# A delta rule with a gated feed-forward behind it, on one core: the same instructions issued in another order

## The chip, the cores and the metric

The kernel runs on one core of a Trainium2 chip. A core has a matrix engine (PE, with PEld for its weight loads), a vector engine (DVE), a scalar engine (ACT), GpSimd (POOL) and a queue engine (SP); DMAs are issued from the streams of SP, ACT and POOL. Every engine takes its instructions in the order in which the program gives them, and waits where one is not ready. The metric is the device time of one execution in microseconds (us); the kernel before takes 507.92 us (median of 3 runs, 506.95 to 509.35).

## The reference

The inputs are q, k, v of shape 4 x 8 x 768 x 48 (batch, head, token, channel) and beta of 4 x 8 x 768. For each of the 32 heads, token by token:

```
k_n = k / (norm(k) + 1e-6);  state = 0
y[t]  = q[t] @ state
state = state + beta[t] * outer(k_n[t], v[t] - k_n[t] @ state)
```

The heads' y, put side by side, is x (4 x 768 x 384). Behind it stands a feed-forward with gating over tokens:

```
h = gelu(x @ w_in)                      # 384 -> 1024; u, v = the two halves of 512
v_n = (v - mean) / sqrt(var + 1e-6) * g_ln
v_s = w_sg @ v_n + b_sg                 # over the 768 tokens
out = x + (u * v_s) @ w_out             # 512 -> 384
```

## The kernel before

The recurrence is worked out in 12 chunks (0 to 11) of 64 tokens: chunks 0 to 5 for two of the batches, 6 to 11 for the other two. Within a chunk one needs the inverse of a triangular 64 x 64 matrix for each head. The program has a step for each piece of work, and the string PROGRAM (lines 47 to 98) names the steps one after the other; the loop at line 1128 calls them, and each engine gets its instructions in just that order. Nothing else sets the order. Of a step `name:a:b` the numbers say which chunk, part or queue; S, A and P are the DMA queues of SP, ACT and POOL.

- **Loads and Gram matrices.** `keys`, `q`, `kt`, `v` load a chunk's arrays; `w:k` loads a piece of w_in (six pieces; the later three are loaded from POOL when an earlier piece is done, line 768). `gram:c` multiplies a chunk's keys with each other (line 129, as all the recurrence's matmuls), and `gstore` sends the result to DRAM (gd).
- **Lanes.** The inverse of the 32 x 32 blocks is made on DVE, row by row, in four groups: group 0 for chunks 0 and 1, group 1 for chunks 2 and 3, group 2 for chunks 4 to 7, group 3 for chunks 8 to 11. `lanes:0` issues the whole of group 0 at once, behind `tin`, which brings the blocks in with a DVE transpose. `bglanes:g` only puts a later group's instructions on a list, and `l:n` issues the next n of them. A group begins with a copy of the diagonal (line 351) and a masking on POOL (line 353); the pairs at lines 407 and 414 are its bulk. `zload` fetches a group's blocks from gd into the one tile zl; at a group's end the result is stored to DRAM (zd, line 461), and `blocks` and `heads` load it back (line 467).
- **Chain of a chunk.** `join`, `corner_a`, `corner_b` put the 32 x 32 blocks together on PE, with ACT copying out of PSUM. Then, twice a chunk (e = 0, 1): `old` (PE; DVE adds to v at line 638 and masks gq at line 322), `own` (PE, ACT), `state` (PE, ACT). The next half needs the state of the one before.
- **Decoding.** w_in arrives as 64-bit words and is taken apart on DVE into a high and a low float: `d:n` issues the next n of 18 parts, three for each of the six pieces, with 4, 3 and 2 DVE instructions and one ACT cast (lines 719 to 737). `gate` needs the first three pieces, `values` all six.
- **First feed-forward.** For each chunk `turn` transposes x, `gate:c:d` makes a quarter of u (9 matmuls, lines 775 to 777, and a gelu on ACT), and `values:c:n` issues the next n of 18 matmuls of v (line 811); at the 9th and the 18th follow the gelu, a store to DRAM (vD) and the moments on DVE. This is the work with which PE can be filled while a chain waits.
- **Weights of the second part.** `late_weights` and 22 `unit` steps load and split w_out and w_sg.
- **Second part.** From `last_part` on: `vload` and `vsplit` load v from vD and normalize and split it (ACT, DVE), `sp` (18 matmuls, then DVE, then POOL) and `gs` (split) do the mixing over tokens, `pj` (12 matmuls) the projection, `xload` and `ost` are its load and store. For batches 1 and 3 the split v is put where winh and winl lie.
- **Warming.** `kick`, `warm` and `wm` issue matmuls whose results nobody reads.

The steps that begin the kernel before, and its third-last stage, read:

```
kick:12 consts beta:P l:7 keys:0:S ... gram:1 w:0:P keys:3:P tin l:12 wm:9:13 d:3 lanes:0 keys:2:A
gram:3 gram:2 ... zload:1:S old:0:0 ... bglanes:1 heads:0 wm:6:7 join:0:0 ...
... unit:1 l:2 values:11:18
vsplit:0:3 unit:1 vsplit:0:4 vsplit:0:5 unit:1 norm ... sp:0:0:0
```

Of the kernel before, what the change touches and what calls it, by code (L numbers as in the profile page):

```python
# [48 lines left out]
gram:3 gram:2 l:3 wm:2:3 gstore:2:S:S q:0:P norms:0 v:0:P vprep:0 q:1:S gstore:3:P zload:1:S old:0:0 keys:4:S keys:5:P
blocks:0:P kt:0:A bglanes:1 heads:0 wm:6:7 join:0:0 keys:7:S join:1:0 turned:0 l:5 l:8 l:1 l:5 blocks:1:P w:2:S gram:4  # L50
gstore:4:S:P w:1:P join:2:0 join:3:0 warm:6 l:8 l:8 heads:1:A corner_a:0 v:1:P l:5 l:7 gram:5 corner_b:0 join:0:1
kt:1:P turned:1 join:1:1 l:5 l:4 keys:6:S d:1 vprep:1 own:0:0 l:12 gstore:5:S:A state:0:0 old:1:0 join:2:1 keys:8:P
own:1:0 d:4 join:3:1 state:1:0 d:1 gram:6 blocks:2:S:S:P zload:2:S corner_a:1 xstore:0 old:0:1 heads:2:S:P join:0:2
corner_b:1 d:1 own:0:1 l:5 d:2 d:1 gram:7 l:2 gstore:6:A:P:A join:1:2 turned:2 l:3 gstore:7:S:P:P d:2 d:1 state:0:1
join:2:2 zload:3:P old:1:1 norms:1 join:3:2 d:2 v:2:S bglanes:2 own:1:1 turn:0 keys:10:A l:6 vprep:2 heads:3:P q:2:S
l:2 gram:8 state:1:1 corner_a:2 gate:0:0 keys:9:A blocks:3:S:S corner_b:2 l:13 old:0:2 l:2 l:1 kt:2:S join:0:3 l:2
join:1:3 turned:3 values:0:4 l:7 values:0:2 own:0:2 values:0:6 xstore:1 values:0:6 gram:9 state:0:2 l:6 turn:1
join:2:3 v:3:P gstore:8:P old:1:2 keys:11:A vprep:3 l:5 gate:0:1 kt:3:P gate:0:2 join:3:3 q:3:A own:1:2 corner_a:3 l:5
values:1:10 values:1:3 state:1:2 xstore:2 l:5 q:4:S values:1:2 gate:1:0 old:0:3 l:1 l:9 corner_b:3 norms:2 gate:0:3
ustore:0 own:0:3 values:1:3 state:0:3 gstore:9:A turn:2 old:1:3 gate:1:1 gate:1:2 kt:4:P v:4:S l:1 gate:1:3 own:1:3  # L60
ustore:1 gram:10 q:5:S gate:2:0 gstore:10:S:A gate:2:1 heads:4:P state:1:3 gram:11 values:2:2 blocks:4:S:A gate:2:2
l:10 gate:2:3 gstore:11:S:P v:5:P zload:4:S vprep:4 values:2:1 turn:3 zload:5:P bglanes:3 values:2:7 blocks:5:S:P
gate:3:0 old:0:4 corner_a:4 values:2:1 values:2:5 turned:4 corner_b:4 values:2:2 heads:5:P gate:3:1 own:0:4 gate:3:2
vprep:5 gate:3:3 ustore:2 state:0:4 l:12 old:1:4 turned:5 corner_a:5 own:1:4 heads:6:S:A:P blocks:6:P v:6:A values:3:1
state:1:4 ustore:3 corner_b:5 values:3:1 l:15 values:3:13 l:1 old:0:5 xstore:4 turn:4 l:4 kt:5:A values:3:2 values:3:1
l:3 kt:6:A own:0:5 turned:6 xstore:3 l:2 values:4:7 values:4:11 state:0:5 norms:3 corner_a:6 vprep:6 old:1:5
heads:7:S:S gate:4:0 corner_b:6 q:6:S own:1:5 norms:4 gate:4:1 blocks:7:S state:1:5 l:11 old:0:6 own:0:6 norms:5
gate:4:2 v:7:S l:1 gate:4:3 turn:5 l:2 state:0:6 turned:7 corner_a:7 l:3 gate:5:0 old:1:6 l:4 ustore:4 l:1 gate:5:1
xstore:5 own:1:6 gate:5:2 q:7:S l:7 l:2 values:5:3 values:5:15 q:8:S vprep:7 l:1 state:1:6 xstore:6 kt:7:A v:8:P
corner_b:7 old:0:7 kt:8:P gate:5:3 ustore:5 turn:6 l:12 blocks:8:S l:7 heads:8:S own:0:7 values:6:18 state:0:7  # L70
gate:6:0 bgnorm old:1:7 gate:6:1 turned:8 vprep:8 own:1:7 gate:6:2 state:1:7 unit:1 corner_a:8 gate:6:3 v:9:P old:0:8
q:9:P corner_b:8 turn:7 own:0:8 gate:7:0 gate:7:1 late_weights heads:9:A l:6 kt:9:S gate:7:2 unit:1 state:0:8
blocks:9:S gate:7:3 old:1:8 turned:9 corner_a:9 own:1:8 heads:10:A values:7:4 ustore:6 ustore:7 unit:1 values:7:4
blocks:10:S:A state:1:8 corner_b:9 vprep:9 v:10:A old:0:9 values:7:6 turn:8 own:0:9 l:1 values:7:3 xstore:7 turned:10
values:7:1 gate:8:0 unit:1 state:0:9 vprep:10 corner_a:10 old:1:9 q:10:S gate:8:1 gate:8:2 heads:11:P:A own:1:9
gate:8:3 unit:1 state:1:9 unit:1 xstore:8 blocks:11:P corner_b:10 ustore:8 turn:9 l:7 kt:10:P old:0:10 values:8:18
own:0:10 values:9:5 unit:1 l:10 v:11:A state:0:10 unit:1 q:11:P turned:11 gate:9:0 xstore:9 old:1:10 gate:9:1 gate:9:2
unit:1 corner_a:11 own:1:10 values:9:6 unit:1 values:9:7 vprep:11 state:1:10 corner_b:11 old:0:11 kt:11:P turn:10
gate:9:3 values:10:5 values:10:4 own:0:11 values:10:3 unit:1 unit:1 l:4 unit:1 state:0:11 values:10:6 old:1:11
xstore:10 gate:10:0 own:1:11 unit:1 gate:10:1 ustore:9 state:1:11 unit:1 xstore:11 turn:11 gate:10:2 gate:10:3 l:15  # L80
gate:11:0 gate:11:1 last_part vload:0:0 vload:0:1 unit:1 l:5 vload:0:2 uload:0:0 vload:0:3 vsplit:0:0 vload:0:4 unit:1
gate:11:2 vsplit:0:1 gate:11:3 vload:0:5 gains unit:1 ustore:11 vsplit:0:2 ustore:10 unit:1 l:2 values:11:18
vsplit:0:3 unit:1 vsplit:0:4 vsplit:0:5 unit:1 norm uload:0:1 vload:1:0 unit:1 vload:1:1 vload:1:2 vload:1:3 sp:0:0:0
sp:0:0:1 gs:0:0:0 vsplit:1:0 vload:1:4 sp:0:0:2 gs:0:0:1 vsplit:1:1 vload:1:5 sp:0:0:3 gs:0:0:2 vsplit:1:2 gs:0:0:3
sp:0:1:0 vsplit:1:3 sp:0:1:1 gs:0:1:0 sp:0:1:2 gs:0:1:1 vsplit:1:4 uload:1:0 sp:0:1:3 vsplit:1:5 gs:0:1:2 xload:0:0
xload:0:1 xload:0:2 gs:0:1:3 pj:0:0 ost:0:0 pj:0:1 ost:0:1 pj:0:2 ost:0:2 vload:2:0 vload:2:1 vload:2:2 l:1 vload:2:3
sp:1:0:0 sp:1:0:1 gs:1:0:0 vsplit:2:0 vload:2:4 sp:1:0:2 gs:1:0:1 vsplit:2:1 uload:1:1 vload:2:5 sp:1:0:3 gs:1:0:2
vsplit:2:2 xload:0:3 xload:0:4 xload:0:5 gs:1:0:3 sp:1:1:0 pj:0:3 ost:0:3 pj:0:4 ost:0:4 pj:0:5 ost:0:5 gs:1:1:0
vsplit:2:3 sp:1:1:1 vsplit:2:4 uload:2:0 gs:1:1:1 sp:1:1:2 vsplit:2:5 sp:1:1:3 gs:1:1:2 xload:1:0 xload:1:1 pj:1:0
ost:1:0 pj:1:1 xload:1:2 gs:1:1:3 pj:1:2 ost:1:1 ost:1:2 uload:2:1 vload:3:0 vload:3:1 vload:3:2 vsplit:3:0 vload:3:3  # L90
sp:2:0:0 sp:2:0:1 xload:1:3 gs:2:0:0 vload:3:4 sp:2:0:2 gs:2:0:1 vsplit:3:1 xload:1:4 sp:2:0:3 vsplit:3:2 gs:2:0:2
vload:3:5 xload:1:5 gs:2:0:3 pj:1:3 ost:1:3 pj:1:4 ost:1:4 pj:1:5 xload:2:0 ost:1:5 sp:2:1:0 vsplit:3:3 sp:2:1:1
gs:2:1:0 vsplit:3:4 uload:3:0 sp:2:1:2 gs:2:1:1 vsplit:3:5 sp:2:1:3 xload:2:1 gs:2:1:2 xload:2:2 gs:2:1:3 pj:2:0
ost:2:0 pj:2:1 ost:2:1 pj:2:2 uload:3:1 ost:2:2 sp:3:0:0 sp:3:0:1 gs:3:0:0 sp:3:0:2 gs:3:0:1 sp:3:0:3 gs:3:0:2
xload:2:3 xload:2:4 xload:2:5 gs:3:0:3 pj:2:3 ost:2:3 pj:2:4 pj:2:5 ost:2:4 ost:2:5 sp:3:1:0 sp:3:1:1 gs:3:1:0
sp:3:1:2 gs:3:1:1 sp:3:1:3 gs:3:1:2 xload:3:0 xload:3:1 xload:3:2 gs:3:1:3 pj:3:0 pj:3:1 ost:3:0 ost:3:1 xload:3:3
pj:3:2 xload:3:4 pj:3:3 xload:3:5 ost:3:2 ost:3:3 pj:3:4 ost:3:4 pj:3:5 ost:3:5
"""


# [1080 lines left out]
```

## Time and profile before

| | |
|---|---|
| median of 3 runs | 507.92 us |
| the profiled execution's own time | 505.82 us |
| its span, first to last instruction | 504.0 us |
| mean granted clock of PE | 0.901 of full speed |
| PE busy | 455.6 us, 90% |
| DVE busy | 335.5 us, 67% |
| ACT busy | 205.9 us, 41% |
| POOL busy | 102.5 us, 20% |

The chain of waits that ended last goes 58% through PE, 23% through DVE, 8% through DMAs and 5% through ACT. A busy PE is not a PE at its peak: where the granted clock is 0.50 the same matmul takes twice as long, and counts as busy all the while. So the stages are read by busy time, clock and number of matmuls together.

### The profile page before, as it was taken

Reading aid. Unit: us, or ns where it says so; the run is one execution under the profiler, and the core shown is the slowest. Engines: PE = TensorE matmul, PEld = TensorE weight load, DVE = VectorE, ACT = ScalarE, POOL = GpSimd, SP = SyncE. Lnnn points to the kernel's source line nnn. Section 1 sums busy time; section 2 is a strip of 40 time slices with the busy share of each in tenths; the row PEclk is TensorE's granted clock in tenths of the full one; section 3 lists DMA queues with packets and bytes.
Section 4 is the critical chain, followed back from the end, with each engine's and each line's share of the span. In section 5 each row is a group of like instructions: output and inputs, shape, how many; then the busy total and the mean of one; then the engine's idle time right before and its main releaser. Section 6 shows DMA issues by size and latency. Waiting matters only on the chain.

```text
span 504.0 us, 16080 instructions
## 1 busy us (share of the span) xinstructions
PE 455.6 (90%) x6823; PEld 405.0 (80%) x6823; DVE 335.5 (67%) x741; ACT 205.9 (41%) x613; POOL 102.5 (20%) x130
## 2 busy tenths in 40 slices
PE   7518878986999898999999999997999999999997
...
PEclk9656657578999998999999999996999999999999
...
GB/s 96 195 263 60 171 89 167 112 167 101 127 183 199 199 232 142 223 127 119 262 226 197 162 233 180 177 208 237 183 117 135 179 127 204 125 111 156 67 29 142
DMA packets 79432, 81.03 MB, mean 161 GB/s; under 512 B 43280, under 2 KB 58336, under 8 KB 79360
## 3 DMA queue, kind: packets, MB, share of 16 engines
...
## 4 chain that ended last, share of the span: by engine, by line
PE 58%; DVE 23%; DMA 8%; ACT 5%; issue 3%; POOL 2%; SPq 1%; ACTq 0%; DVEq 0%; POOLq 0%
PE ps L129 16%; PE ps L775 11%; PE ps L777 11%; PE ps L776 11%; PE ps L811 6%; DVE ztmp L407 4%; DVE zl L414 4%; DMA ut<-w_in 2%; ACT gq L639 1%; DMA raw<-w_sgT 1%; DMA gd<-gk 1%; DVE bs L823 1%; DVE gq L322 1%; PE ps L146 1%; DVE zl L383 1%
## 5 line engine op out<-in xcount | busy, mean ns | idle before, releaser
L912 POOL TENSOR_TENSOR ga<-ga,uT 128x384 f32<-128x384 f32 x32 | 36.6, 1146 | 140.4 <-DVE ga L909 88.1
L780 ACT CAST gh<-ga 128x384 fp32r<-128x384 f32 x32 | 16.4, 512 | 95.3 <-POOL ga L912 90.0
L775 PE MATMUL ps<-xh,winh 128*128 128x256 f32 x144 | 43.5, 302 | 2.1 <-DVE xl L801 1.1
L776 PE MATMUL ps<-xl,winh 128*128 128x256 f32 x144 | 40.9, 284 | 0.4 <-DVE xl L801 0.3
L777 PE MATMUL ps<-xh,winl 128*128 128x256 f32 x144 | 40.6, 282 | 0.0
L909 DVE SCALAR_TENSOR_TENSOR ga<-ps,g_sb,bsg_bc 128x384 f32<-128x384 f32 x32 | 19.6, 615 | 29.7 <-PE ps L777 29.6
L414 DVE TENSOR_TENSOR zl<-zl,ztmp 128x28 f32<-128x28 f32 (+20 forms) x84 | 36.0, 428 | 2.6
L407 DVE TENSOR_TENSOR ztmp<-zl 128x28 f32<-128x28 f32 (+20 forms) x84 | 35.9, 427 | 2.5
L129 PE MATMUL ps<-v,z 64*64 64x48 f32 x768 | 33.0, 239 | 4.5 <-ACT gq L639 1.7
L775 PE MATMUL ps<-wsgh,vnh 128*128 128x384 f32 x96 | 34.3, 358 | 3.0 <-ACT vnh L890 3.0
L129 PEld LDWEIGHTS ps<-v,z 64*64 64x64 f32 x768 | 29.1, 152 | 9.7 <-issue 4.2
L777 PE MATMUL ps<-wsgh,vnl 128*128 128x384 f32 x96 | 34.3, 357 | 0.6 <-DVE vnl L894 0.6
L811 PE MATMUL ps<-winh,xh 128*128 128x512 f32 x72 | 30.7, 426 | 4.2 <-ACT jy L541 4.0
L776 PE MATMUL ps<-wsgl,vnh 128*128 128x384 f32 x96 | 34.0, 354 | 0.0
L776 PE MATMUL ps<-woutl,gh 128*128 128x384 f32 x96 | 32.5, 339 | 0.0
L775 PE MATMUL ps<-wsgh,winh 128*128 128x384 f32 x96 | 32.5, 339 | 0.0
L775 PE MATMUL ps<-wouth,gh 128*128 128x384 f32 x96 | 32.5, 339 | 0.0
L777 PE MATMUL ps<-wouth,gl 128*128 128x384 f32 x96 | 32.5, 339 | 0.0
L777 PE MATMUL ps<-wsgh,winl 128*128 128x384 f32 x96 | 32.5, 339 | 0.0
L776 PE MATMUL ps<-wsgl,winh 128*128 128x384 f32 x96 | 32.5, 339 | 0.0
L775 PEld LDWEIGHTS ps<-xh,winh 128*128 128x128 f32 x144 | 27.4, 190 | 5.3 <-ACT xh L798 1.4
L129 PE MATMUL ps<-qs,k 48*64 48x128 f32 (+1 forms) x768 | 28.4, 291 | 1.3 <-issue 0.7
...
## 6 DMA issues: line engine op xcount, KB each, us to landing
...
```

The source lines that it names most:

```text
L129: return nc.tensor.matmul(out=out, lhsT=lhsT, rhs=rhs, start=start, stop=stop, skip_group_check=True)
L146: nc.tensor.matmul(out=ps, lhsT=lhsT, rhs=busy, start=True, stop=True)
L322: nc.vector.tensor_tensor(out=m, in0=m, in1=later.unsqueeze(1).broadcast_to([P, 8, T]), op=ALU.mult)
L407: tv.tensor_tensor(out=products(i, r0, r1, at), in0=zb[:, :, r0:r1, i:i + 1].broadcast_to([P, nblk, r1 - r0, w]), in1=zb[:, :, i:i + 1, i ...
L414: tv.tensor_tensor(out=z_, in0=z_, in1=products(i, r0, r1, at), op=ALU.add)
L775: nc.tensor.matmul(out=ps, lhsT=sh, rhs=mh, start=(first and i == 0), stop=False)
L776: nc.tensor.matmul(out=ps, lhsT=sh, rhs=ml, start=False, stop=False)
L777: nc.tensor.matmul(out=ps, lhsT=sl, rhs=mh, start=False, stop=(last and i == n - 1))
L780: nc.scalar.copy(out=hi, in_=src)
L811: nc.tensor.matmul(out=self.ps, lhsT=(self.xl if k == 2 else self.xh)[:, cc, bi], rhs=(winl if k == 1 else winh)[:, cc, DH:], start=(i == ...
L909: nc.vector.scalar_tensor_tensor(out=ga, in0=ps, scalar=g_sb[:, d:d + 1], in1=bsg_bc[:, hs], op0=ALU.mult, op1=ALU.add)
L912: nc.gpsimd.tensor_tensor(out=gv, in0=gv, in1=uxs[b, th][:, :, d], op=ALU.mult)
```

## The change

Only the string PROGRAM is replaced; it is 11 lines longer, so that a line n of the kernel before is line n + 11 after it. The same functions are called, with the same matmuls: 12 kicks, 29 other warming matmuls, all grams, chains, gates and values are there in equal number. What changes is where each stands, and from which queue many loads and stores go: 44 DMAs are issued from ACT (32 before), 62 from POOL (73), 279 from SP (280). Lanes 1 to 3 are issued in 98 `l` steps (60 before), 44 of them of a single instruction; the 216 matmuls of `values` in 125 steps (38 before), 76 of them single.

```
--- before.py
+++ after.py
@@ -45,56 +45,67 @@
 PROGRAM = """
-kick:12 consts beta:P l:7 keys:0:S l:2 l:3 gram:0 keys:1:S gram:1 w:0:P keys:3:P tin l:12 wm:9:13 d:3 lanes:0 keys:2:A
...
+keys:0:S consts keys:1:S keys:3:S gram:0 q:1:P keys:2:S gram:1 w:1:A w:0:S kick:12 beta:P keys:4:S tin lanes:0
...
```

**DVE at the start.** Before, from the transpose that brings in the blocks of chunks 0 and 1 (zl) to the first instruction of lane group 0 (rsq_y); ut and vg are the raw and the decoded piece of w_in, winl its low part:

```order
L264 STREAM_TRANSPOSE zl<-g_103 128x32x32
L719 TENSOR_SCALAR vg<-ut 128x512
L720 TENSOR_SCALAR vg<-ut 128x512
L723 SCALAR_TENSOR_TENSOR vg<-ut,vg 128x512
L725 SCALAR_TENSOR_TENSOR vg<-vg 128x512
L730 TENSOR_SCALAR vg<-vg 128x512
L731 SCALAR_TENSOR_TENSOR ut<-ut,vg 128x512
L733 TENSOR_TENSOR ut<-ut,vg 128x512
L736 TENSOR_TENSOR vg<-vg,winh 128x512
L737 SCALAR_TENSOR_TENSOR winl<-ut,vg 128x512
L214 TENSOR_SCALAR rsq_y_287<-d_283 128x32
```

Now, at the same place on DVE:

```order
L275 STREAM_TRANSPOSE zl<-g_103 128x32x32
L225 TENSOR_SCALAR rsq_y_266<-d_262 128x32
L230 SCALAR_TENSOR_TENSOR rsq_t_267<-d_262,rsq_y_266 128x32
L232 TENSOR_TENSOR rsq_t_267<-rsq_t_267,rsq_y_266 128x32
L233 SCALAR_TENSOR_TENSOR rsq_y_266<-rsq_t_267,rsq_y_266 128x32
```

The nine decoding instructions are gone from between. They come behind group 0, in parts, and between them the first instructions of lane group 1 (the copy into d_412, and rsq); DVE from the last transpose of group 0 on (gk is where its result goes, gq the masked product of chunk 0):

```order
L467 STREAM_TRANSPOSE gk_109<-zl 128x32x32
L730 TENSOR_SCALAR vg<-ut 128x512
L731 TENSOR_SCALAR vg<-ut 128x512
L734 SCALAR_TENSOR_TENSOR vg<-ut,vg 128x512
L736 SCALAR_TENSOR_TENSOR vg<-vg 128x512
L362 COPY d_412<-zl 128x32
L333 TENSOR_TENSOR gq_110<-gq_110,later 128x512
L225 TENSOR_SCALAR rsq_y_413<-d_412 128x32
L741 TENSOR_SCALAR vg<-vg 128x512
L742 SCALAR_TENSOR_TENSOR ut<-ut,vg 128x512
L744 TENSOR_TENSOR ut<-ut,vg 128x512
```

So a piece is decoded in three portions, with lanes between them, from the end of group 0 on.

**PE where the second part begins.** Before, the last values (L811) are followed by the first mixing matmuls (wsgh, wsgl: w_sg split; vnh, vnl: v normalized and split), and none comes back:

```order
L811 MATMUL ps<-winh,xh 128x512
L811 MATMUL ps<-winl,xh 128x512
L811 MATMUL ps<-winh,xl 128x512
L775 MATMUL ps<-wsgh,vnh 128x384
L776 MATMUL ps<-wsgl,vnh 128x384
L777 MATMUL ps<-wsgh,vnl 128x384
```

Now, PE at the end of the first mixing step (18 matmuls, L786 to L788) has one of the matmuls of values (L822), then the next mixing step begins; seven of them stand so between mixing steps:

```order
L787 MATMUL ps<-wsgl,vnh 128x384
L788 MATMUL ps<-wsgh,vnl 128x384
L822 MATMUL ps<-winh,xl 128x512
L786 MATMUL ps<-wsgh,vnh 128x384
```

**ACT at the hand-over from lane group 2 to group 3.** Now the loads of group 2's result (zk and z from zd) and of group 3's blocks (zl from gd) are issued in the ACT stream, among the gelus of the gates (ut):

```order
L843 ACTIVATE ut<-ps 128x2x2x64 x2
L478 DMA zk_2498<-zd 128x4x32 x2
L843 ACTIVATE ut<-ps 128x2x2x64
L340 DMA zl<-gd 128x1024
L478 DMA z_114<-zd 32x16x32
L843 ACTIVATE ut<-ps 128x2x2x64 x2
```

Before, ACT held two loads of z there, and the load of zl went from SP and POOL:

```order
L467 DMA z_114<-zd 32x16x32 x2
L832 ACTIVATE ut<-ps 128x2x2x64 x2
L798 CAST xh<-ps 128x3x128 x2
L817 ACTIVATE vg<-ps 128x512
```

Two more loads that wait for a store thus stand ahead of ACT's own work.

## Rows read from the trace of the kernel before

**Rows 1.** The page: PE's busy time, and PE and its clock in 40 slices.

```profile
PE 455.6 (90%) x6823; PEld 405.0 (80%) x6823; DVE 335.5 (67%) x741; ACT 205.9 (41%) x613; POOL 102.5 (20%) x130
...
PE   7518878986999898999999999997999999999997
...
PEclk9656657578999998999999999996999999999999
```

**Rows 2.** By stage: PE, PEld, DVE, ACT, POOL busy us, clock, DMA share, GB/s.

```profile
36.00:110.00 74.00, 63.81 (x1148) 53.63 (x1152) 46.92 (x113) 33.84 (x127) 19.25 (x28) 0.62 0.48 127
110.00:168.00 58.00, 51.86 (x1209) 45.02 (x1202) 51.69 (x111) 31.50 (x106) 10.19 (x13) 0.93 0.60 160
168.00:186.00 18.00, 16.66 (x210) 14.02 (x211) 7.45 (x16) 8.34 (x25) 7.15 (x11) 1.00 0.84 226
186.00:247.00 61.00, 57.31 (x1224) 48.30 (x1225) 55.85 (x118) 32.96 (x109) 6.29 (x8) 0.97 0.55 170
247.00:336.00 89.00, 88.37 (x1858) 75.77 (x1857) 56.71 (x160) 53.05 (x161) 6.87 (x10) 1.00 0.68 197
336.00:348.00 12.00, 8.38 (x32) 6.20 (x31) 9.56 (x19) 6.55 (x12) 0.00 (x0) 0.80 0.91 248
348.00:360.00 12.00, 12.00 (x55) 11.64 (x55) 5.60 (x20) 2.73 (x5) 2.25 (x2) 0.77 0.82 244
...
349.00:500.00 151.00, 151.00 (x845) 151.00 (x844) 79.45 (x135) 29.40 (x50) 36.62 (x32) 0.99 0.45 133
```

**Rows 3.** DVE in order of time: start us, us, instruction [idle before, releaser].

```profile
14.51 0.43 DVE L719 TENSOR_SCALAR vg<-ut 128x512 int32<-128x512 int32 x1 [1.12 <-DMA ut<-w_in]
...
20.81 0.17 DVE L214 TENSOR_SCALAR rsq_y<-d 128x32 int32<-128x32 int32 x1
...
33.74 2.00 DVE L456 STREAM_TRANSPOSE gk<-zl 128x1024 f32<-128x1024 f32 x1
...
110.19 0.21 DVE L351 COPY d<-zl 128x64 f32<-128x64 f32 x1
...
185.48 0.22 DVE L351 COPY d<-zl 128x64 f32<-128x64 f32 x1 [1.01 <-DMA zl<-gd]
```

**Rows 4.** PE in order of time, the first grams (two, then one).

```profile
5.94 2.10 PE L129 MATMUL ps<-k 48*64 48x64 f32 x128
...
15.82 2.10 PE L129 MATMUL ps<-k 48*64 48x64 f32 x64 [4.88 <-DMA k<-kT]
```

**Rows 5.** By stage, lane group 0 alone; columns as in rows 2.

```profile
20.80:35.75 14.95, 4.79 (x100) 3.33 (x100) 13.30 (x50) 2.48 (x9) 3.18 (x5) 0.50 0.96 260
```

**Rows 6.** The chain that ended last, between lane groups 2 and 3.

```profile
166.57 1.24 DVE zl L383
...
167.89 3.59 DMA zd<-zl
171.56 2.65 DMA z<-zd
174.21 6.09 DMA gd<-gk
...
181.03 4.42 DMA zl<-gd
```

**Rows 7.** ACT and PE in order of time, at the second part's start.

```profile
343.25 0.81 ACT L890 ACTIVATE vnh<-vraw,nrb 128x512 fp32r<-128x512 f32 x1 [2.86 <-DMA vraw<-vD]
...
344.12 0.69 PE L775 MATMUL ps<-wsgh,vnh 128*128 128x384 f32 x1 [3.02 <-ACT vnh L890]
```

**Rows 8.** Waits: total us, times, longest us.

```profile
DVE v L638 <- PE ps L129: 15.7, 7, 5.1
...
DVE bs L823 <- ACT vg L817: 12.1, 8, 3.7
...
DVE gq L322 <- ACT gq L639: 9.9, 22, 0.5
...
ACT ut L832 <- DMA zd<-zl: 3.7, 1, 3.7
```

More of the change, by code (lines that the diff above doesn't have):

```diff
@@ L47 @@
 PROGRAM = """
-kick:12 consts beta:P l:7 keys:0:S l:2 l:3 gram:0 keys:1:S gram:1 w:0:P keys:3:P tin l:12 wm:9:13 d:3 lanes:0 keys:2:A
[L49 to L97, printed above, removed]
+keys:0:S consts keys:1:S keys:3:S gram:0 q:1:P keys:2:S gram:1 w:1:A w:0:S kick:12 beta:P keys:4:S tin lanes:0
@@ new lines @@
+keys:6:P gram:3 v:0:A q:0:P gram:2 d:1 gstore:2:A:P:P gstore:3:P:A:S zload:1:S bglanes:1 l:1 old:0:0 l:1 blocks:0:A
+wm:6:7 wm:9:13 heads:0 join:1:0 d:1 norms:0 l:2 turned:0 l:1 join:0:0 keys:8:P l:1 join:2:0 d:1 join:0:1 l:3 vprep:0
+l:8 gram:4 l:2 d:1 l:1 corner_a:0 join:3:0 l:2 keys:7:S heads:1 turned:1 v:1:A l:3 kt:1:A keys:5:S d:1 l:1 vprep:1
+warm:6 l:6 kt:0:P l:1 gram:5 d:1 l:3 corner_b:0 l:1 blocks:1:S:S:S:P l:6 join:1:1 gram:8 l:1 own:0:0 state:0:0 l:3
+join:2:1 wm:2:3 gstore:4:P:S:S old:1:0 gram:7 gstore:5:S:S:P w:2:S d:1 l:1 heads:2:S join:3:1 d:1 own:1:0
@@ new lines @@
+blocks:2:A:A:S:A gram:6 state:1:0 d:2 corner_a:1 old:0:1 turned:2 gstore:6:A:S:P d:2 corner_b:1 join:0:2
+gstore:7:S:A:S own:0:1 zload:2:P state:0:1 d:2 join:1:2 old:1:1 zload:3:P xstore:0 d:1 join:2:2 own:1:1 d:1 norms:1
+keys:10:P state:1:1 d:1 v:2:P d:1 corner_a:2 bglanes:2 l:1 turn:0 join:3:2 l:1 values:0:2 l:1 turn:1 l:2 q:2:P kt:2:S
+gate:0:0 values:1:1 l:3 gate:0:2 heads:3:S vprep:2 l:2 gate:1:0 l:4 turned:3 l:3 blocks:3:S:P:P:A l:2 norms:3
+corner_b:2 q:3:S old:0:2 l:6 values:0:1 l:5 values:0:1 l:1 values:0:1 kt:3:A values:0:1 own:0:2 norms:2 values:0:4
@@ new lines @@
+state:0:2 values:1:3 l:1 keys:9:P join:0:3 l:1 join:1:3 values:1:3 v:3:A gstore:8:A:A:P l:2 old:1:2 l:3 values:1:1
+gate:1:3 values:1:1 l:3 own:1:2 q:4:A v:4:S values:0:4 l:1 values:0:1 l:1 values:0:1 l:1 values:0:1 l:2 vprep:3
+xstore:1 l:1 values:0:1 join:2:3 state:1:2 keys:11:A corner_a:3 gate:1:2 gate:0:3 l:1 xstore:2 join:3:3 l:1 old:0:3
+gram:10 corner_b:3 gate:0:1 l:5 own:0:3 l:1 turn:2 l:4 state:0:3 l:2 gram:11 l:2 old:1:3 l:2 values:2:1 l:1 values:2:1
+values:1:2 values:2:1 values:1:3 l:2 values:1:1 l:1 gstore:10:S:P:P l:4 values:2:1 l:4 ustore:0 kt:4:P gate:1:1 l:2
@@ new lines @@
+values:2:3 gstore:11:P ustore:1 own:1:3 values:1:2 v:5:P values:1:1 gram:9 gstore:9:A:P:S state:1:3 gate:2:0 gate:2:3
+turn:3 gate:2:2 gate:2:1 values:3:3 vprep:5 l:1 heads:4:A gate:3:0 zload:4:A zload:5:P vprep:4 values:3:1
+blocks:4:S:S:P:A values:3:1 gate:3:3 gate:3:1 old:0:4 turned:4 corner_a:4 bglanes:3 l:1 values:2:2 l:2 values:3:3
+corner_b:4 heads:5:S values:3:1 blocks:5:P:P:S:A values:3:1 values:2:1 l:5 values:2:2 own:0:4 l:1 kt:5:P values:2:1
+q:5:P values:2:1 turned:5 state:0:4 l:6 values:2:1 values:3:2 old:1:4 values:3:2 l:2 values:2:1 heads:6:S:P l:2
@@ new lines @@
+values:2:2 own:1:4 l:4 v:6:S l:1 corner_a:5 state:1:4 kt:6:S gate:3:2 turn:4 ustore:2 l:1 old:0:5 values:4:2 l:1 q:6:S
+vprep:6 values:4:1 l:2 values:3:1 l:2 values:3:1 values:4:4 blocks:6:P:P:P:S values:4:1 turned:6 l:2 values:3:2 l:4
+values:4:1 xstore:4 l:2 corner_b:5 corner_a:6 own:0:5 gate:4:0 gate:4:1 xstore:3 corner_b:6 old:0:6 state:0:5 norms:5
+l:2 own:0:6 l:1 old:1:5 state:0:6 l:1 values:4:4 l:1 own:1:5 l:1 old:1:6 l:2 blocks:7:P:S:S:S state:1:5 kt:7:S
+gate:4:2 values:4:1 turn:5 heads:7:P:A gate:4:3 v:7:P ustore:4 values:4:1 values:5:1 l:5 own:1:6 l:1 values:5:1 q:8:S
@@ new lines @@
+values:5:1 values:4:3 state:1:6 corner_a:7 xstore:6 gate:5:0 values:5:1 l:1 turned:7 xstore:5 values:5:3 q:7:P l:2
+values:5:1 l:3 gate:5:2 ustore:3 l:2 turn:6 l:3 gate:5:1 values:6:1 gate:5:3 values:6:3 ustore:5 vprep:7 l:1 kt:8:A
+l:3 norms:4 corner_b:7 old:0:7 l:12 values:6:3 v:8:A values:5:2 values:6:1 values:5:5 values:6:1 own:0:7 gate:6:0
+gate:6:2 state:0:7 gate:6:3 old:1:7 l:1 blocks:8:S:A:P:A gate:6:1 own:1:7 values:5:3 bgnorm l:1 state:1:7 heads:8:P
+vprep:8 turn:7 l:3 corner_a:8 values:7:4 blocks:9:P:S:A:P turned:8 old:0:8 v:9:P vprep:9 corner_b:8 corner_a:9 own:0:8
@@ new lines @@
+q:9:P values:7:2 values:6:1 heads:9:S gate:7:0 turned:9 state:0:8 corner_b:9 late_weights unit:1 heads:10:S old:1:8
+values:7:1 xstore:7 gate:7:3 unit:1 kt:9:A values:6:1 own:1:8 blocks:10:A:A:A:S values:6:5 unit:1 state:1:8 values:6:2
+turn:8 l:1 old:0:9 l:1 xstore:8 values:7:2 values:8:3 values:7:1 values:8:3 own:0:9 q:10:P values:7:1 unit:1 l:1
+values:7:1 gate:7:2 ustore:6 v:10:P unit:1 values:7:3 state:0:9 corner_a:10 turned:10 old:1:9 values:8:3 heads:11:P:S
+values:7:1 gate:7:1 gate:8:0 gate:8:1 values:7:1 unit:2 own:1:9 corner_b:10 blocks:11:S:P:S:A v:11:A state:1:9
```

25 lines of the change are left out of this document (added).

## Prediction, before the changed kernel had run

> **What bounds the kernel now.** I read the page first, then the stages, then DVE in order of time, and the chain and the waits last. PE is busy 455.6 us, but its clock stands near 0.6 in several of the first ten slices and near full speed nearly everywhere later [rows 1], so a busy PE means different things early and late. The stages say it in numbers [rows 2]. From 349 to 500 PE is busy all of 151.00 us at a clock of 0.99, in 845 matmuls, so 0.179 us each: no order of the same matmuls makes this shorter. From 247 to 336 it is busy 88.37 of 89. From 36 to 110 it is busy 63.81 of 74 at 0.62 only, while DVE is busy 46.92: there neither engine is the limit, but a chain that goes back and forth between them. From 336 to 360, where the second part begins, PE gets through 32 + 55 = 87 matmuls, and at 0.179 us it would get through 134.
>
> What is to be shortened is thus the start, up to 110, where lane group 2 begins on DVE [rows 3], and the passage at 336 to 360. Lane group 2 is the mark because groups 2 and 3 are DVE's long work, and the stages behind hang on them: group 2 ends at 167.8, and group 3 begins only at 185.48 [rows 3, 6].
>
> **Part A: decoding goes behind lane group 0.** Nine decode instructions stand from 14.51 to 20.81 between the transpose of the blocks and lane group 0, 6.3 us, and the first waits 1.12 for its piece of w_in [rows 3]: 7.4 us between the transpose's end and group 0. All of it leaves the path. What stays is a copy of the diagonal (such copies take 0.2 [rows 3]) and its hand-over, 0.4 together. What comes in: the 12 kicks now stand behind the first two grams, so these run at the low clock. Today both, 128 matmuls, take 2.10 us; the next gram, 64 matmuls, takes 2.10 as well [rows 4], so at that clock the two would take 4.2. That costs up to 2.1, or nothing if the copies behind them cover it; I take 1.1, the middle. The sum is 7.4 − 0.4 − 1.1 = 5.9, bounds 7.0 and 4.9. Group 0 ends at 33.74 + 2.00 = 35.74 now [rows 3], and then at 29.8.
>
> **Part B: what lies between group 0 and group 2.** The decoding isn't gone, it moves into this stretch. DVE was busy 46.92 from 36 to 110 [rows 2], so it has 46.92 + 6.3 = 53.2 to do there. How densely it can do so I take from group 0 alone, where DVE is busy 13.30 of 14.95 [rows 5], a ratio of 1.124: 53.2 × 1.124 = 59.8, so group 2 could begin at 29.8 + 59.8 = 89.6. That supposes that DVE always has something ready, which single lane instructions between the chain's joins are able to give: while DVE waits today for a product of PE or a copy of ACT, as in the rows of waits for v and gq [rows 8], a ready lane instruction can stand there. The other end is that the chain keeps its idle time and the decoding merely fills or lengthens it: then the 74 us stay, the 6.3 come on top, and group 2 begins at 110.1, no gain. PE sets a nearer bound: its 63.81 busy us of this stretch, at today's low clock, end at 29.8 + 63.8 = 93.6 if it doesn't idle. More activity should lift the clock above 0.62, since in the stages where PE idles less the rows show 0.93 and more [rows 2], but not wholly. I take 91, between the two: a gain of 110.2 − 91 = 19 with part A (bounds 0 and 110.2 − 89.6 = 20.6, or 21.7 if the grams cost nothing).
>
> **Part C: from group 2 to the end of values.** Here PE's idle time is 6.1 (110 to 168), 1.3 (168 to 186), 3.7 (186 to 247) and 0.6 (247 to 336), 11.7 in all; the clocks of 0.93 and 0.97 cost about 3.6 and 1.7 [rows 2]. Nothing beyond 17 us can come from here. Between the groups DVE waits 17.7 us for a round through DRAM: store zd 3.59, load z 2.65, a store of gd that lands after 6.09, load zl 4.42 [rows 6]. An order that sends gd earlier could leave about the 3.59 + 2.65 + 4.42 = 10.7 of the others, but PE is busy 16.66 of those 18 us, so that only shifts the lanes. Against it, ACT now holds the loads of z and of zl in its own stream, and each waits for a store: 3.59 and 6.09, up to 9.7 us in which the gelus behind them stand, and PE behind those, whose PSUM they empty. Its row today is one such wait of 3.7, of ut for zd [rows 8]. In between I take a gain of 3 (bounds: 17 gained, 9.7 lost). The gain that B makes is kept through this part only because its stages are PE's: PE works through the same matmuls 19 us earlier.
>
> **Part D: the passage to the second part.** PE lost (134 − 87) × 0.179 = 8.4 us there; some of the first 32 matmuls write 512 columns, not 384, so say 7.5. The reason is that mixing waits 3.02 for ACT's vnh, and this 2.86 for vraw, which comes back from DRAM [rows 7]. Seven held-back matmuls of values between mixing steps and more gates ahead can lie in that hole: 7 × 0.179 × 512/384 = 1.7, and as much again for a gate of 9. I take 4 (bounds 0 and 7.5).
>
> **Part E: the rest.** The mixing and projecting from 360 on is the same PE work at 0.99: 0, within 1 on either side. The exchanged DMA queues I price at nothing while the DMA share is about half [rows 2]; where it is 0.84 to 0.91 they can't help.
>
> The sum against the profiled execution's own 505.82: −19 − 3 − 4 = −26, so 479.8. The median of the runs lies 2.1 above that execution; I put half of it on, 481. With 3 us of error on B, 7 on C and 3 on D, the forecast's own range is 470 to 490.
>
> **Rivals.** *The chain keeps half of its idle time.* The joins and old/own/state of a half wait for each other in turn, and lanes in between can delay a join as well as fill its wait. For it: PE and DVE are both half idle today though lanes were there to issue. Then half of B's 13 beyond A is lost and some of A is eaten by the decoding: group 2 at 102, 8 gained, C nothing, D 4: 12 in all, 505.8 − 12 + 1 = 495.
>
> *ACT stands on its loads.* Loads of z and of heads now stand in ACT's stream at three places before and between the groups, and one of zl: 3 × 3.7 + 6.09 = 17 us [rows 6, 8] of ACT, and if PE waits for all of it the 26 shrink to 9: 505.8 − 9 + 1 = 498. Against it: ACT is busy 41% [rows 1], so much of a wait is caught up. The Trainium skill, page "DMA: Bandwidth & Descriptors", section "Anatomy of one DMA — SWDGE (gpsimd) path", says that DMA engines do not wait on semaphores; the wait happens on the issuing sequencer, before dispatch. The trace agrees, since ACT idled 3.7 us before a gelu for the store of zd [rows 8]. By that rule the full 17 us would be paid by ACT, and by the row's one wait, which is in ACT's idle 59%, little of it: the rule speaks for this rival.
>
> *Single instructions cost hand-overs (slower).* In lane groups 2 and 3, 43 steps of one instruction now stand between steps of the chain, so DVE changes between lanes and a result of PE or ACT 43 times, in order, and whichever isn't ready holds the other. Today the waits of this kind are 15.7 in 7, 12.1 in 8 and 9.9 in 22 [rows 8], 37.7 in 37, about 1.0 us each. If each change costs over 26 / 43 = 0.6 us on the path that ends last, the gain is gone; at 0.8 it is 34, so 481 + 34 = 515, slower. Against it: DVE is idle a third of the time, and PE, not DVE, is full from 186 on [rows 2].
>
> *The first loads collide.* The pieces of w_in now go ahead on SP and ACT beside four keys; in group 0's time the DMAs' share is 0.96 already [rows 5]. If the blocks land that much later, A is gone, and B with it in its part that stands on A; with C and D at half, 3.5, it is 505.8 − 3.5 + 1 = 503, a little under no change.
>
> **How the numbers follow.** Chances: the forecast 0.58, the chain 0.20, ACT 0.08, hand-overs 0.09, collision 0.05. About 0.5%, 2.5 us, is what a measurement of this kernel can tell from no change. Forecast, chain and ACT are faster save for a small part of each, 0.84 in all; the collision, which with a little less of C is within the bound, and the edges make 0.06 same; hand-overs and the edges on their side 0.10 slower. The range reaches from 467 (the forecast with 14 more of its bounds in B, C and D) to 504, which takes in both faster rivals and leaves out the slower one and a little of the collision.
>
> **What would show it.** Right: DVE begins group 0 at about 15 (20.81) and ends it at about 30; group 2 begins at about 91 (110.19) with DVE denser than 46.92 of 74, and PE's clock over 0.62 in that stretch; group 3 begins at 160 to 165 (185.48); the last stage's 845 matmuls take the same 151 us; the hole before mixing is about half. The chain's rival shows as group 2 at 100 or later, with waits of v for PE as long as now. ACT's shows as waits of ut for zd or gd of some us with PE waiting for PSUM. The hand-overs' shows as lanes of groups 2 and 3 that take longer than 57.6 and 61 with many short waits of DVE. The forecast is wrong if group 2 begins early but the end of values doesn't move with it: then PE's work behind was not what bound those stages.

## The result, and the profile after

The changed kernel takes 474.94 us (median of 4 runs, 472.36 to 477.15), the kernel before 507.62 (median of 4). The ratio is 0.935, 95% interval 0.930 to 0.940: 33 us faster, where 27 were forecast. The profiled execution is the slowest of the four, 477.15 us with a span of 475.4, so its own difference to before (505.82) is 28.7. In the experiments below, runs more than 1.5% above the fastest of their kernel are left out of the median.

The page after; PE's busy time, and PE and its clock in 40 slices:

```profile
PE 440.9 (93%) x6823; PEld 392.2 (82%) x6823; DVE 324.7 (68%) x741; ACT 205.1 (43%) x613; POOL 92.5 (19%) x119
...
PE   5378989989999999999999999989999989999996
...
PEclk9875796789999999999999999989999999999999
```

The same 6823 matmuls, 14.7 us less busy time [rows 1]: of the 28.6 us that the span is shorter, about half is idle time, the other half busy time, with the mean clock at 0.947 instead of 0.901. DVE after, in order of time (start, us, instruction): the first instruction of lane group 0, its last transpose, the first of group 2, the last two of group 2 (one line, x2), the first of group 3.

```profile
13.82 0.18 DVE L225 TENSOR_SCALAR rsq_y<-d 128x32 int32<-128x32 int32 x1 [0.31 <-ACT d L362]
...
27.91 2.05 DVE L467 STREAM_TRANSPOSE gk<-zl 128x1024 f32<-128x1024 f32 x1
...
94.33 0.21 DVE L362 COPY d<-zl 128x64 f32<-128x64 f32 x1
...
147.40 2.36 DVE L394 TENSOR_TENSOR zl<-zl,nb 128x1024 f32<-128x1024 f32 x2
...
159.85 0.22 DVE L362 COPY d<-zl 128x64 f32<-128x64 f32 x1 [1.13 <-DMA zl<-gd]
```

Against [rows 3] group 0 ends 5.8 us earlier (35.74 to 29.96), group 2 begins 15.9 earlier (110.19 to 94.33), group 3 begins 25.6 earlier (185.48 to 159.85). The first mixing matmul of before and of after, from PE in order of time:

```profile
339.35 0.34 PE L775 MATMUL ps<-wsgh,vnh 128*128 128x384 f32 x1
```

```profile
310.08 0.34 PE L786 MATMUL ps<-wsgh,vnh 128*128 128x384 f32 x1
...
314.22 0.44 PE L787 MATMUL ps<-wsgl,vnh 128*128 128x384 f32 x1 [1.35 <-DVE wsgl L792]
...
316.50 0.52 PE L786 MATMUL ps<-wsgh,vnh 128*128 128x384 f32 x1
```

It comes 29.3 earlier, and the span ends 28.6 earlier. So all of the gain is there before mixing begins; about half by group 2's beginning and nearly half after it. The stages after, cut at those marks (columns as in rows 2):

```profile
30.00:94.30 64.30, 56.45 (x1242) 48.57 (x1243) 50.08 (x119) 38.71 (x147) 10.90 (x15) 0.73 0.57 142
94.30:149.80 55.50, 51.63 (x1121) 44.31 (x1121) 51.47 (x113) 30.49 (x99) 13.07 (x18) 0.97 0.66 169
149.80:159.90 10.10, 9.81 (x107) 8.56 (x107) 5.09 (x11) 4.68 (x16) 1.24 (x2) 1.00 0.79 238
159.90:220.10 60.20, 59.86 (x1336) 50.50 (x1335) 55.36 (x121) 35.33 (x111) 10.65 (x14) 1.00 0.67 196
220.10:310.00 89.90, 88.40 (x1843) 75.12 (x1835) 60.67 (x169) 54.29 (x162) 7.71 (x11) 1.00 0.70 204
```

From group 2 to the first mixing (the last four lines), PE idles 3.9 + 0.3 + 0.3 + 1.5 = 6.0 us, where it idled 11.7 [rows 2], and its clock is full from 150 on. DVE is busy 50.08 of 64.3 from 30 to 94 instead of 46.92 of 74, the decoding among it. The hand-over between groups 2 and 3 takes 159.85 − 149.76 = 10.1 us. Before, the last two instructions of group 2, at the same place on DVE, were

```profile
166.57 2.36 DVE L383 TENSOR_TENSOR zl<-zl,nb 128x1024 f32<-128x1024 f32 x2
```

so it was 185.48 − 168.93 = 16.6 (the prediction counted from the first of the two, 17.7). What makes it up; issues on the queues in order of time, before and after:

```profile
167.89 1.97 SPq L461 DMA_DIRECT2D zd<-zl  x2
...
172.40 1.03 SPq L308 DMA_DIRECT2D gd<-gk  x2
```

```profile
145.53 1.32 POOL L319 DMA_DIRECT2D gd<-g  x2 [1.91 <-ACT g L302]
...
148.69 1.45 SPq L472 DMA_DIRECT2D zd<-zl  x2
...
153.56 0.34 ACTq L340 DMA_DIRECT2D zl<-gd  x1
...
154.04 0.57 POOL L340 DMA_DIRECT2D zl<-gd  x1 [7.20 <-DMA zd<-zl]
```

Before, the last stores of gd were issued behind the store of zd; now they stand ahead of it. So the load of zl no longer waits for one of them (6.09 us in [rows 6]), but for the store of zd.

### The profile page after: what moved, and what is told of

Same layout as the page of the kernel before. It is cut to its first block, busy times and chain, and to the rows that moved or that the text cites. A ratio compares the mean times of both kernels' runs of the same rounds, so it can differ in the third digit from the quotient of the medians.

```text
span 475.4 us, 16073 instructions
## 1 busy us (share of the span) xinstructions
PE 440.9 (93%) x6823; PEld 392.2 (82%) x6823; DVE 324.7 (68%) x741; ACT 205.1 (43%) x613; POOL 92.5 (19%) x119
## 4 chain that ended last, share of the span: by engine, by line
PE 44%; DVE 28%; DMA 10%; ACT 8%; issue 4%; SPq 3%; POOL 1%; ACTq 1%; DVEq 0%; POOLq 0%
PE ps L140 18%; PE ps L786 7%; PE ps L788 7%; PE ps L787 6%; PE ps L822 5%; DVE zl L425 4%; DVE ztmp L418 4%; DMA vraw<-vD 3%; DMA uT<-uD 2%; DMA kt<-ktok 2%; SPq L896 2%; ACT gq L650 1%; DVE bs L834 1%; DVE vraw L903 1%; POOL ga L923 1%
## 5 line engine op out<-in xcount | busy, mean ns | idle before, releaser
L923 POOL TENSOR_TENSOR ga<-ga,uT 128x384 f32<-128x384 f32 x32 | 34.3, 1079 | 166.9 <-DVE ga L920 92.1
L786 PE MATMUL ps<-xh,winh 128*128 128x256 f32 x144 | 43.2, 300 | 0.0
L788 PE MATMUL ps<-xh,winl 128*128 128x256 f32 x144 | 40.8, 284 | 0.0
L140 PE MATMUL ps<-qs,k 48*64 48x128 f32 (+1 forms) x768 | 27.0, 281 | 8.1 <-DMA qs<-qT 8.0
L788 PE MATMUL ps<-wsgh,vnl 128*128 128x384 f32 x96 | 33.4, 348 | 0.8 <-DVE vnl L905 0.7
L792 DVE TENSOR_TENSOR gl<-ga,gh 128x384 fp32r<-128x384 f32 x32 | 18.7, 588 | 22.0 <-ACT gh L791 22.0
L786 PE MATMUL ps<-wouth,gh 128*128 128x384 f32 x96 | 32.6, 340 | 0.9 <-ACT gh L791 0.9
L786 PE MATMUL ps<-wsgh,vnh 128*128 128x384 f32 x96 | 33.3, 346 | 0.2 <-ACT vnh L901 0.2
L788 PE MATMUL ps<-wouth,gl 128*128 128x384 f32 x96 | 32.6, 340 | 0.0
L140 PEld LDWEIGHTS ps<-v,z 64*64 64x64 f32 x768 | 25.8, 138 | 8.1 <-issue 3.5
L788 PE MATMUL ps<-wsgh,winl 128*128 128x384 f32 x96 | 32.5, 339 | 0.0
L786 PE MATMUL ps<-wsgh,winh 128*128 128x384 f32 x96 | 32.5, 339 | 0.0
L140 PEld LDWEIGHTS ps<-qs,k 48*64 48x64 f32 x768 | 21.3, 140 | 12.4 <-issue 9.4
L140 PE MATMUL ps<-v,z 64*64 64x48 f32 x768 | 29.4, 224 | 1.7 <-ACT z L604 0.5
```

The source lines that it names most:

```text
L140: return nc.tensor.matmul(out=out, lhsT=lhsT, rhs=rhs, start=start, stop=stop, skip_group_check=True)
L786: nc.tensor.matmul(out=ps, lhsT=sh, rhs=mh, start=(first and i == 0), stop=False)
L788: nc.tensor.matmul(out=ps, lhsT=sl, rhs=mh, start=False, stop=(last and i == n - 1))
L792: nc.vector.tensor_tensor(out=lo, in0=src, in1=hi.bitcast(F32), op=ALU.subtract)
L923: nc.gpsimd.tensor_tensor(out=gv, in0=gv, in1=uxs[b, th][:, :, d], op=ALU.mult)
```

## The experiments

Each is compared by its median with 474.94 (the changed kernel) or with the kernel before as it ran beside it (506 to 507).

**Only the start new.** The string up to `bglanes:2` is the changed kernel's, the rest that of before.

```
  ... state:1:1 d:1 v:2:P d:1 corner_a:2
- bglanes:2 l:1 turn:0 join:3:2 l:1 values:0:2 l:1 turn:1 l:2 q:2:P ...
+ join:3:2 bglanes:2 turn:0 l:6 vprep:2 heads:3:P q:2:S l:2 gate:0:0 ...
```

> The changed kernel's order up to the start of lane group 2, and from there the order of the kernel before. The theory, that the start gives 16 us (lane group 2 begins at 94.3 instead of 110.2) and that what follows keeps it because PE is full there, expects 507.6 - 16 = 492 us, with lane group 2 at 94 to 95. The rival, that the early start only moves the wait to the hand-over between lane groups 2 and 3 and into values, so that it needs the new order behind it, expects 500 us or more.

Measured: 488.1 us, ratio to before 0.965 (0.960 to 0.971), 18 us gained. Group 2 begins at 91.28 on DVE, group 3 at 167.18, where the changed kernel has 159.85:

```profile
91.28 0.21 DVE L351 COPY d<-zl 128x64 f32<-128x64 f32 x1
...
167.18 0.22 DVE L351 COPY d<-zl 128x64 f32<-128x64 f32 x1 [0.71 <-DMA zl<-gd]
```

The start keeps its gain to the end behind the old order; the rival falls.

**Only the rest new.** The reverse cut.

> The other half: the order of the kernel before up to the start of lane group 2, then the changed kernel's. The theory expects the remaining 13 us of the profiled difference: 507.6 - 13 = 494 us, with the hand-over between lane groups 2 and 3 at about 10 us instead of 17.7. The rival, that the later order gives nothing by itself, expects 505 us or more.

Measured: 498.7 us (496.3 to 500.7), ratio 0.986 (0.979 to 0.993), 7.5 gained, between the two expectations. Group 2 begins at 110.59 as before, ends at 169.21 + 2.36 = 171.57 and group 3 begins at 180.97: a hand-over of 9.4 with the old start in front.

```profile
110.59 0.22 DVE L360 COPY d<-zl 128x64 f32<-128x64 f32 x1
...
169.21 2.36 DVE L392 TENSOR_TENSOR zl<-zl,nb 128x1024 f32<-128x1024 f32 x2
...
180.97 0.22 DVE L360 COPY d<-zl 128x64 f32<-128x64 f32 x1
```

The two halves give 18.1 and 7.5, together 25.6 of the 31 to 33. The rest, some 6 us, seems to come only when both are there; with an interval of about 3 us on either side of each half, its size is uncertain.

**The decoding back ahead of lane group 0.**

```
- beta:P keys:4:S tin lanes:0 ... gram:2 d:1 ... join:1:0 d:1 ... join:2:0 d:1
+ beta:P keys:4:S tin d:3 lanes:0 ... gram:2 ... join:1:0 ... join:2:0
```

> The changed kernel with the first three decoding parts (nine DVE instructions) back in one piece between the transpose and lane group 0. The theory, that these stand on the path which sets the start, expects lane group 0 to end 6 to 7 us later, lane group 2 to begin as much later, and 475 + 6 = 481 us. The rival, that DVE's idle time between 30 and 94 us (14 of 64) takes them up, expects lane group 2 within 2 us of 94.3 and 475 to 477 us.

Measured: 481.7 us (480.8 to 483.1), 6.7 slower than the changed kernel. Group 0 begins at 19.38, ends at 34.31 and group 2 begins at 96.02. The stretch between, by stage, and below it the same stretch in the kernel with values before mixing (told further down), which has the changed kernel's start and nearly the same granted clock (0.82; the changed kernel's own profile has 0.73 there):

```profile
34.30:96.00 61.70, 52.95 (x1240) 45.37 (x1240) 45.26 (x111) 37.34 (x145) 10.69 (x15) 0.81 0.56 144
```

```profile
29.70:90.40 60.70, 51.76 (x1227) 43.99 (x1227) 50.17 (x120) 37.18 (x144) 10.86 (x15) 0.82 0.58 143
```

The stretch is as long with the nine instructions in it (DVE busy 50.17) as without (45.26): behind group 0 they cost nothing. Ahead of it they cost most of their 6.3 us: group 0 ends 4.3 us later than in the changed kernel (6 to 7 were expected), and group 2 begins about 5 us later than the 90.4 to 91.3 of other executions with this start at a clock of 0.82 or 0.83. It begins only 1.7 later than the 94.3 of the changed kernel's own profile, as the rival had expected; the median of 481.7 decides for the theory.

**Only the stretch between lane groups 1 and 2 new.** From `bglanes:1` to `bglanes:2` the changed order, before and behind it the old one.

> The order of the kernel before, with the changed kernel's only between the start of lane group 1 and that of lane group 2 (decoding still ahead of lane group 0). The prediction split the 19 us of the start into 5.9 for the decoding and 13 for the denser stretch behind it. If the stretch is worth its part by itself: 506 - 13 = 493 us, with lane group 2 at about 97. The rival, that decoding ahead of group 0 is what the whole start hangs on, expects lane group 2 at 105 or later and 501 us or more.

Measured: 493.0 us (491.6 to 498.1), ratio 0.977 (0.967 to 0.986), so 12 to 13 gained. In the profiled execution, the slowest of these at 498.1, group 2 begins at 102.6 (its copy of the diagonal), 7.6 earlier than before: between the two expectations, while the time meets the first. The denser stretch is worth some 10 by itself, with the decoding still ahead.

**Values in nines, all chunks.** Each nine at the place of its ninth matmul.

```
- l:6 values:0:1 l:5 values:0:1 l:1 values:0:1 kt:3:A values:0:1 own:0:2 norms:2 values:0:4
+ l:6 l:5 l:1 kt:3:A own:0:2 norms:2 values:0:9
```

The last nines of chunks 10 and 11 here read halves of w_in where steps of the second part have already written, so those values are not the reference's; the times are of the same instructions.

> The changed kernel with the matmuls of values issued nine at a time, each nine at the place where its ninth stood; lanes, chains, gates and stores stay. The theory, that single matmuls of values fill PE's waits from 94 us on (idle there 6.0 us against 11.8, and the clock higher), expects the idle time and clock of the kernel before in those stages, +9 us: 484. The rival, that their size does not matter since whole nines fill as well, expects 474 to 477.

Measured: 492.8 us (491.1 to 494.4), 18 slower, twice what was expected; in the profiled execution mixing begins 6 us later than in the changed kernel's, and the rest of the way takes 9.5 us more, where the last nines stand between mixing steps. So it was done again **in nines for chunks 0 to 8 only**:

> The changed kernel with values in nines for chunks 0 to 8 only; chunks 9 to 11, which reach into the passage, keep their ones and twos. In the nines run over all chunks the passage and the stretch before it lost most. If the small pieces matter in the passage alone, this is 475 to 478 us; if they matter in the chains' stretches too (idle 6.0 us from 94 to 310 against 16.4 with nines), 480 to 484.

Measured: 482.1 us (479.2 to 483.4), 7 slower. By stage, groups 2 and 3 and the values behind them:

```profile
90.60:147.60 57.00, 48.86 (x1109) 42.49 (x1108) 51.42 (x113) 30.30 (x99) 13.03 (x18) 0.97 0.63 163
...
157.50:219.80 62.30, 60.65 (x1356) 51.82 (x1352) 55.40 (x121) 35.29 (x111) 10.63 (x14) 1.00 0.63 190
219.80:314.60 94.80, 90.73 (x1825) 77.69 (x1826) 61.26 (x169) 55.26 (x163) 7.69 (x11) 0.98 0.67 194
```

PE idles 8.1, 1.7 and 4.1 us in them, against 3.9, 0.3 and 1.5 in the changed kernel. Ones and twos of values fill PE's waits; nines leave them open. A nine also stands later than its first eight matmuls did, so size and place are changed together.

**Lanes in tens.** The 98 steps of lanes become 19, each where ten or more instructions have come together.

```
- gram:4 l:2 d:1 l:1 corner_a:0 join:3:0 l:2 keys:7:S ... l:3 kt:1:A ... l:1 vprep:1 warm:6 l:6
+ gram:4 d:1 corner_a:0 join:3:0 keys:7:S ... kt:1:A ... vprep:1 warm:6 l:15
```

> The changed kernel with the lanes of groups 1 to 3 issued in 19 steps of ten or more instructions in place of 98 small ones, each at the place of its last. If single lane instructions cost hand-overs (0.3 us each would be 13 us), this is faster, 462 to 470 us. If they fill the chain's waits, as the prediction has it, this is slower: chain steps wait behind blocks of 10 x 0.4 = 4 us of lanes, 482 to 490.

Measured: 527.1 us (523.5 to 528.9), ratio to before 1.048 (1.037 to 1.058): 52 slower than the changed kernel, far more than the 482 to 490 expected, and slower than before. Waits of PE in lane group 3's stretch (total, times, longest), and the stretch:

```profile
PE ps L136 <- DVE xl L808: 4.2, 1, 4.2
PE ps L136 <- DVE v L645: 3.1, 1, 3.1
```

```profile
182.20:261.80 79.60, 66.47 (x1280) 56.55 (x1279) 56.69 (x117) 33.04 (x106) 9.32 (x12) 0.87 0.46 140
```

PE waits for DVE results that stand behind a block of lanes, idles 13.1 of 79.6 and drops to a clock of 0.87; with small steps it is 59.86 of 60.2 at 1.00. The longer wait ends behind a block of lanes on DVE from 224.06 to 230.72, with xl right after it. In this kernel small steps gain far more than their hand-overs cost. Here too the lanes are issued later as well as in larger blocks.

**The old queues in the new order.** Only letters change, 69 words.

```
- gstore:2:A:P:P ... blocks:4:S:S:P:A ... zload:4:A ... blocks:8:S:A:P:A
+ gstore:2:S:S ... blocks:4:S:A ... zload:4:S ... blocks:8:S
```

> The changed kernel with every DMA on the queues of the kernel before; only the queues change, no order. The theory that queues are worth nothing expects 475 us within 2. The rival that ACT loses time on the loads it now holds expects a gain, 465 to 470. The other rival, that the new queues carry part of the gain (stores spread over three queues, so that a hand-over takes 10 and not 17.7 us), expects 480 or more.

Measured: 490.0 us (486.2 to 493.1), 15 slower. The last two instructions of group 2 and the first of group 3; waits of PE at the hand-over, of DVE near 240, and the windows with the clock there:

```profile
148.51 2.36 DVE L392 TENSOR_TENSOR zl<-zl,nb 128x1024 f32<-128x1024 f32 x2
...
162.52 0.22 DVE L360 COPY d<-zl 128x64 f32<-128x64 f32 x1 [1.94 <-DMA zl<-gd]
```

```profile
PE ps L138 <- DMA z<-zd: 4.1, 1, 4.1
```

```profile
DVE ztk L514 <- DMA zk<-zd: 8.4, 1, 8.4
```

```profile
160.00:170.00 10.00, 7.57 (x78) 5.69 (x82) 2.17 (x7) 4.02 (x12) 5.24 (x6) 0.66 0.30 85
...
240.00:250.00 10.00, 7.52 (x160) 6.55 (x162) 1.59 (x5) 3.83 (x15) 0.68 (x1) 0.79 0.77 220
```

The loads of z and zk come late, PE idles, and its clock falls for a while behind. The changed kernel's list of waits has neither. The hand-over takes 162.52 − 150.87 = 11.7 us, 1.6 more than with the new queues and 5 less than before: most of its shortening is the order's, not the queues'. Group 3 begins 2.7 us later than in the changed kernel, the first mixing matmul (327.19) 17 us later, so the loss lies mostly behind group 3's beginning.

**The old queues for these loads alone** (`blocks`, 12 words):

> The changed kernel with only the loads of the lanes' result (zk and z from zd, twelve steps blocks) on the queues of the kernel before, mostly one queue for four loads. With all old queues PE waited 5.0 us for z from zd, 4.1 of it between lane groups 2 and 3. If these loads are what the queues are worth, this is 484 to 491 us with those waits; if the other loads and stores are, 475 to 479.

Measured: 478.2 us (475.1 to 481.7), 3 of the 15. The same two waits here:

```profile
PE ps L138 <- DMA z<-zd: 3.5, 2, 2.5
```

```profile
DVE ztk L514 <- DMA zk<-zd: 0.2, 1, 0.2
```

Of PE's wait for z most is back, DVE's wait for zk is not: that one came with other loads and stores. They hold the rest of the 15, and which of them stays open.

**The new queues in the old order.**

> The kernel before, in its own order, with every load and store on the queues of the changed kernel. With the old queues the changed kernel lost 17 us. If the new queues (stores and loads of one piece spread over up to four queues) are better for any order, the kernel before gains by them: 506 - 8 or more, 490 to 498 us. If queues and order only fit each other, it gains nothing or loses: 504 to 515.

Measured: 517.9 us, ratio 1.020 (1.015 to 1.025), 10.8 slower than before. Waits of PE that are longer (1.1 for u before) or new (x at L775):

```profile
PE ps L129 <- ACT u L661: 5.9, 3, 4.8
...
PE ps L775 <- ACT x L688: 3.6, 1, 3.6
```

The new queues aren't better, they fit the new order and harm the old one.

**The held-back values in front of mixing.** The seven single matmuls move ahead of `sp:0:0:2`.

> The changed kernel with the seven held-back matmuls of values in front of the first mixing step. The prediction gave the passage 4 us, the trace shows some 1.7 (7 x 0.24). If they fill a wait, this is 476 to 479 us, with the wait for wsgl or vnh longer by as much; if they fill nothing, 475 within 1.

Measured: 474.1 us (472.0 to 476.9, 6 runs), the changed kernel's time. The first 10 us of mixing, and mixing with all behind it:

```profile
312.00:322.00 10.00, 10.00 (x58) 10.00 (x57) 5.28 (x12) 2.44 (x5) 0.00 (x0) 1.00 0.76 191
...
312.00:469.40 157.40, 154.10 (x865) 152.06 (x863) 78.95 (x146) 30.22 (x54) 34.23 (x32) 1.00 0.46 139
```

No wait at mixing's beginning and a full clock. The held-back values give nothing that the median shows.

**An attempt to improve.** Four `unit` steps earlier, and `wm:0:9` (nine warming matmuls) in front of `join:0:0`, where PE idles and its clock falls.

> The changed kernel with two edits: four of the unit steps that split w_sg stand some chunks earlier, and nine warming matmuls lie in PE's idle 2.36 us after 32.0, where its clock falls to half until 52. If both do what they say, the wait of 1.35 us for wsgl and the low clock behind it go (2 to 3 us), and PE's 18 busy us at half clock shrink by some (2 to 5 us): 468 to 472. If the chain and not PE's clock sets that stretch, and units earlier delay lanes, 474 to 478.

Measured: 477.0 us (477.0 to 481.4, three of six runs): not the 468 to 472 of the first expectation, and no clear difference from 474.94. The profiled execution took 487.9, so its trace doesn't explain that median. PE in it, in order of time:

```profile
33.66 3.30 PE L155 MATMUL ps<-busy 128*128 128x512 bf16 x9 [1.95 <-ACT jy L550]
36.89 1.58 PE L138 MATMUL ps<-gk,g 32*128 32x128 f32 x16
```

The warming matmuls didn't lie in the gap; they waited for the same ACT result as the join, and the join, at 34.40 in the changed kernel, begins at 36.89 in this execution, 2.5 us later. The two edits weren't run apart, so what the units did stays open. No version here is clearly faster than the changed kernel.

## Why the prediction was right, step by step

**Part A held.** 5.9 was forecast for group 0's end, 5.8 measured, and putting the decoding back costs 4.3 there and 6.7 in the median. That the sum is met so closely is luck, for two errors cancel in it: the grams behind late kicks cost nothing (the transpose is over by 13.51, as before within 0.2), and group 0 itself takes 16.1 instead of 14.9.

**Part B held.** Group 2 was forecast at 91; it begins at 94.3 in the profiled execution and at 90.4 to 91.3 in executions of other kernels with the same start. The difference goes with PE's clock in that stretch, 0.73 in the one, 0.82 or 0.83 in the others; why it differed stays open. Of the bounds, PE's (93.6) was the nearer: DVE is busy 50.08 of 64.3 us, less densely than in group 0. The argument, that DVE can take the decoding in its waits, is shown by the equal stretches with and without it (60.7 and 61.7). The chain's rival (group 2 at 102) falls; it would have been near the truth for the stretch alone (102.6), since part A is missing there. Its premise, that both engines are half idle, misread [rows 2]: of 74 us PE idled 10.2 and DVE 27.1.

**Part C was mis-sized.** 3 us were forecast, and from group 2's beginning to the first mixing matmul it is 29.3 − 15.9 = 13.4. Nearly 6 of it are idle time of PE, nearly 4 the clock (before, 0.93 and 0.97 cost 5.3; now 0.97 costs 1.5). The rest is work that stands elsewhere: 7 × 0.24 = 1.7 for the seven values that come later, and 89 matmuls more are now done before group 2 begins (1562 against 1473). The step that failed is the sentence that a shorter hand-over "only shifts the lanes" because PE is busy 16.66 of 18 us: it became 6.5 us shorter, group 2 itself 3.3 shorter, so group 3 gains another 9.7 on top of group 2's lead, and PE's idle time behind it went from 3.7 to 0.3. No run shortens the hand-over alone, so its own share is not shown. PE's idle time and clock were named as the limit of 17, and what fills them, ones and twos of values, is worth 7 (nines to chunk 8).

**The queues, priced at nothing, were the second failure.** On the new order the old queues cost 15, mostly in C, behind group 3's beginning; so much of C's gain hangs on them, at least as a fit of queue to order. The share of busy DMA engines, on which the price rested, didn't show it: PE and DVE waited 4.1 and 8.4 us for single loads that came late. Which transfers delayed them is only partly known.

**Part D** was put at 4 for the passage. From the first mixing matmul to the span's end it is 164.7 us before and 165.3 after, seven matmuls more: 1.0 gained, and 3.0 with the values ahead (its span of 473.7 − 312.0 = 161.7). The cause given was half wrong: holding values back gives nothing; what goes is the wait for vnh (3.02 in [rows 7]; after, 0.2 for vnh and 1.35 for wsgl). The loads and splits of v stand further ahead now, which fits, but no run moves them back alone.

**The rivals.** Of the loads on ACT little reached PE between group 2 and mixing, where PE idles 6.0 us in all and no wait of ACT for a load from zd or gd is left. It did reach PE at the start, where the prediction didn't look. Four loads of z are issued from ACT there, and its next copy (jy), for which the second join waits, stands behind them. ACT's queue and PE in the changed kernel, then PE in the run with the old queues for `blocks`, where these four go from POOL:

```profile
29.99 3.08 ACTq L478 DMA_DIRECT2D z<-gk  x4
...
34.40 2.18 PE L140 MATMUL ps<-gk,g 32*128 32x128 f32 x16 [2.36 <-ACT jy L552]
```

```profile
32.78 2.18 PE L138 MATMUL ps<-gk,g 32*128 32x128 f32 x16 [1.08 <-ACT jy L550]
```

PE waits 2.36 us for ACT in the one and 1.08 in the other, so ACT's loads cost the chain 1.3 us. Lanes in larger blocks cost 52 us where the rival of the hand-overs had a gain; it also counted 43 single steps in groups 2 and 3, and there are 34 (44 with group 1). The collision of the first loads didn't come: group 0 begins 7 us earlier.

In all 26 were forecast by the profile's own sum, and 28.7 were measured there: C with its queues, 9 too small without the seven values, was made up in part by B, 3 too large in this execution, and by D, 3 too large. That the sum is right within 3 us is thus luck in part: the mechanism of A and B is shown, but C gave about four times what was put down. Of the 6 us between 481 and the measured 474.94 these 2.7 are one part; the rest is that the profiled execution before lay below its median, the one after above it.
